# Retention and a cosine-gated MLP in one kernel: S, Y and A issued as one block on quarters of the array, later blocks with swapped key halves, and a reordered plan

## The chip, the core and the metric

The kernel runs on one core of a Trainium2 chip. The metric is the device time of the kernel in microseconds, as the median of several runs; lower is better. The profile is one further execution, recorded by the hardware.

## What is computed

q, k and v have 4 batches, 8 heads, 768 positions and 64 features. Each head keeps a 64x64 state that decays by a factor gamma at each position:

```python
for t in range(S):
    state = gamma[None, :, None, None] * state + np.einsum('bhd,bhe->bhde', k[:, :, t], v[:, :, t])
    y[:, :, t] = scale * np.einsum('bhd,bhde->bhe', q[:, :, t], state)
```

The result, as 3072 tokens of 512 features, goes through an MLP: `h = x @ w_in` (512 to 2048), `g = h * cos(h)`, `g @ w_out` (2048 to 512).

## The kernel before

**Tiling.** The sequence is cut into chunks of 128 positions. One position p of the kernel is one chunk of two batches, with all eight heads; there are 12 of them, p = 0 to 11, in the order of `ORDER`. Within a chunk the recurrence becomes matrix products: A (keys times queries, then masked so that a query sees no later key), Y (what the state before the chunk gives, plus values times masked A), and S (the state after the chunk, keys times values). Decay is put into q and v by the factors `gq` and `gk` at their conversion to bf16. Two positions make 512 tokens, a group g; six groups go through the MLP in units: an F unit (4 matmuls with 128 hidden features, `f_mm` L472; `h_mm` L493 does the same for 256 tokens and 256 features), its cosine on ScalarE (`f_cos` L480), its product on VectorE (`f_mul` L484, `h_mul` L501), and O units of four matmuls (`o_mm` L517).

**Block of a position.** `y1_mm` issues the state part of Y (L428) and the first half of the rest (`intra`, L414): keys 64 to 127 of batch 1 on the upper row half of the array, keys 0 to 63 of batch 0 on the lower. `hop` (L437) puts an empty instruction on another engine, SP up to p=5 and POOL after, that waits for this half and lets the other half follow[...]. Then come A of the next position (`a_mm` L366), the second half of Y (`y2_mm`) and S (`s_mm`, L460); in the plan at p=2 and 3 A stands apart and S comes before the second half. A and Y use quarters of the array (64 rows, 64 columns); S uses all 128 rows and half of the columns. A's second key half is computed for all 128 queries, Y's second key half for the last 64 only. ScalarE copies Y to `xt` (`y_copy`), VectorE copies the state (`s_copy`) and masks A (`a_mask`, L372).

**Order.** All instructions are ordered by hand. Up to position 5 and the first group's outputs a `Plan` orders them: each operation is added with its engines, its estimated cost, what it comes after, a rank and the tokens (PSUM banks, semaphores) that it takes and gives; `Plan.run` simulates the engines, taking the ready operation of the lowest rank, and `emit` issues the operations in the order of the simulated starts. `jitter` adds random amounts to the ranks. `HALF0` is how many of the 16 hidden blocks of the first group are computed per position rather than for both at once. `LOADS` is the order in which POOL issues the loads, each 512 KB of q, k, v or the weights. After the plan a loop goes over groups g = 2 to 6 and 16 steps: an F unit of group g, an O unit of group g-1, and at the fourth and twelfth step the block of a position, then `conv` of p+2 (keys on ScalarE, queries and values on POOL) and loads of p+4 on SP. Positions from 6 on are transposed by DMA on SP (`dma_t`, L326), the others on TensorE (`t_mm`, L337). There are seven PSUM banks, taken in turn, and one for the state. The last 128 tokens' output is computed in two halves of 256 columns (`last_o`, L537), one copied by ScalarE and one by VectorE.

Of the kernel before, what the change touches and what calls it, by code (L numbers as in the profile page):

```python
# [29 lines left out]
class Plan:  # L30
# [33 lines left out]
    def run(self, start, cold_until=0.0, look=0.0, fill=None, hold=""):  # L64
# [7 lines left out]
        while left:  # L72
            nxt = []
            for e in "SPADE":
# [6 lines left out]
                for op in left:  # L81
# [12 lines left out]
                    for k, n in op["take"]:  # L94
                        tk = sorted(self.tokens[k])
                        n += op["spare"] if k == "bank" else 0
                        if len(tk) < n:
                            ok = False
                        elif tk[n - 1] > t + 1e-9:
                            nxt.append(tk[n - 1])  # L100
                            ok = False
# [50 lines left out]
    def jitter(self, seed, by):  # L152

        r = random.Random(seed)
        for op in self.ops:
            op["rank"] += by * r.random()
# [6 lines left out]
SEED, JIT, HOLD = 60, 4.0, "PD"  # L163
HALF0, SPARE, RF, RM, COLD = 4, 1, 40.0, 40.0, 5.2
# [3 lines left out]
def kernel(  # L168
# [11 lines left out]
    C = 128  # L180
# [12 lines left out]
    ORDER = [0, NC] + [x for x in range(1, NP) if x != NC]  # L193
    LATE = NC
# [39 lines left out]
    mask = sb([128, 128], BF16, "mask")  # L234
# [3 lines left out]
    gk = sb([128, NC, H], FP32, "gk")  # L238
# [27 lines left out]
    def load(eng, p, names):  # L266

        bp, c = divmod(ORDER[p], NC)
        for n in names.split():
            t, src = SRC[n[0].lower()]  # L270
            if len(n) == 1:
# [4 lines left out]
                        "b h t d -> t (b h) d"))  # L276
            else:
# [33 lines left out]
    def conv_v(p, b, e):  # L311
        ENG[e].tensor_tensor(out=vb(p)[:, b], in0=vf[p % PRE][:, b],  # L312
                             in1=bc(gk, ORDER[p] % NC), op=ALU.mult)
# [39 lines left out]

    def a_mm(p, u):
        n = p % NB
        bk = held["a", p, u] = [banks.take(), banks.take()]
        ap = [t.rearrange("p (a t) -> p a t", a=HP) for t in bk]
        for a in range(HP):
            h = 4 * u + a
            for x in range(1 if p < 2 else 2):  # L360
                for b in range(2):
                    if p < 2:
                        nc.tensor.matmul(ap[b][:, a, :], lhsT=kt(n, b, h), rhs=qt(n, b, h),
                                         tile_position=(64 * b, 0))
                        continue
                    nc.tensor.matmul(ap[b][ts(x, 64), a, :], lhsT=kt(n, b, h)[:, ts(x, 64)],  # L366
                                     rhs=qt(n, b, h), tile_position=(64 * b, 64 * x),
                                     skip_group_check=True)

    def a_mask(p, b, u):  # L370
# [3 lines left out]
            in1=(dec[:, b] if p < 2 else mask.unsqueeze(1).to_broadcast([128, HP, 128])),  # L374
# [34 lines left out]
    def intra(p, b, a, x, **kw):  # L409

        ms = []
        for j in range(2):
            h = 2 * a + j
            ms.append(nc.tensor.matmul(  # L414
# [473 lines left out]
```

## Time and profile before

| | us |
|---|---|
| median of 7 runs | 210.26 |
| lowest, highest | 209.81, 211.09 |
| the profiled execution's own time | 210.37 |
| its span, first to last instruction | 208.6 |

Where the engines' work lies, from the groups of instructions:

| line, engine | what | count | mean ns |
|---|---|---|---|
| L472 PE | F units, 512 wide | 289 recorded | 379 |
| L517 PE | O units, 512 wide | 360 recorded | 379 |
| L493 PE | half F units, 256 wide | 160 | 273 |
| L366 PE | A | 320 | 218 |
| L414 PE | Y, values times A | 320 | 205 |
| L428 PE | Y, from the state | 160 | 222 |
| L460 PE | S | 160 | 199 |
| L480 ACT | cosines | 96 | 690 |
| L484 DVE | products | 76 | 688 |
| L372 DVE | masks | 46 | 679 |

A matmul's length in the profile runs from its start to its modelled end and overlaps those of its neighbours; starts of consecutive 512-wide ones lie 216 ns apart. In group rows the last numbers are the busy time, the mean length of one, and the idle time before it with what ended it. Some matmul records are missing, so counts can fall short of the program's.

### The profile page before, as it was taken

To read this page: it belongs to the slowest core of one execution; us is meant where nothing else is said; L and a number is where in the kernel's file an instruction comes from. 1 tells how busy PE (TensorE), PEld (TensorE's weight loads), DVE (VectorE), ACT (ScalarE), POOL (GpSimd) and SP (SyncE) were. 2 spreads that over 40 slices of the span, in tenths; PEclk is the share of its full clock that TensorE was granted. 3 is DMA by queue.
4 is the path that set the end of the run, shared out by engine and by line. 5 is a ranking of instruction groups with operands and counts; after the bars stand their busy time and mean duration, and the time that the engine had idled before them with its cause. 6 is when DMAs were issued, how large, how long until landed. Compare 5 with 4: busy or idle time off the path is not lost.

```text
span 208.6 us, 4799 instructions
## 1 busy us (share of the span) xinstructions
PE 201.4 (97%) x1994; PEld 108.9 (52%) x2017; DVE 107.7 (52%) x186; ACT 116.0 (56%) x194; POOL 80.0 (38%) x84
## 2 busy tenths in 40 slices
PE   7999999999999999999999999999999999999993
PEld 2447456789555545455455455454444444444462
DVE  5374988977725647438438438338332334443000
ACT  7677788579655456556556556554545553553120
POOL 8789989999999007007007007000000000000000
PEclk9999999999999999999999999999999999999999
DMA  7999999999999699999993502401101101110222
GB/s 121 186 258 227 306 248 294 207 335 343 342 290 175 158 234 204 249 220 236 210 265 39 173 0 54 150 0 57 50 3 50 50 10 44 50 50 21 79 79 76
DMA packets 57495, 32.05 MB, mean 154 GB/s; under 512 B 46592, under 2 KB 51968, under 8 KB 57472
## 3 DMA queue, kind: packets, MB, share of 16 engines
q0 software_dynamic: 14352, 15.47, 33.6%
q1 hardware_dynamic: 42976, 16.13, 32.6%
q8 instruction: 16, 0.26, 0.5%
q10 hardware_dynamic: 144, 0.13, 0.2%
q14 instruction: 7, 0.06, 0.1%
HBM read 27.26 MB, written 6.29 MB: 161 GB/s over the span
## 4 chain that ended last, share of the span: by engine, by line
PE 91%; DMA 4%; POOL 2%; issue 1%; DVE 0%; POOLq 0%; DVEq 0%
PE bank L517 38%; PE bank L472 31%; PE bank L493 8%; DMA vf<-in_v_dram 4%; PE bank L366 3%; PE bank L414 2%; PE st_ps L460 2%; PE bank L337 2%; PE bank L537 2%; PE bank L428 2%; PE bank L546 1%; POOL ks L273 1%; PE bank L395 1%; POOL qs L273 1%; POOL kx L273 1%
## 5 line engine op out<-in xcount | busy, mean ns | idle before, releaser
L480 ACT ACTIVATE cosb<-bank,halfpi 128x512 bf16<-128x512 f32 x96 | 65.6, 690 | 57.2 <-PE bank L472 46.2
L517 PE MATMUL bank<-w_out_sb,gt 128*128 128x512 bf16 x360 | 90.1, 379 | 0.9 <-issue 0.3
L484 DVE TENSOR_TENSOR gt<-bank,cosb 128x512 bf16<-128x512 f32 x76 | 51.6, 688 | 55.3 <-ACT cosb L480 55.3
L472 PE MATMUL bank<-xt,w_in_sb 128*128 128x512 bf16 x289 | 74.9, 379 | 0.6 <-issue 0.2
L517 PEld LDWEIGHTS <-gt 128*128 128x128 bf16 x368 | 35.6, 98 | 42.3
L472 PEld LDWEIGHTS <-w_in_sb 128*128 128x128 bf16 x304 | 29.0, 98 | 33.8
L308 POOL TENSOR_TENSOR qs<-qf,gq 128x512 bf16<-128x512 f32 x18 | 18.5, 1044 | 45.0 <-PE bank L414 44.9
L372 DVE TENSOR_TENSOR am<-bank,mask 128x512 bf16<-128x512 f32 x40 | 24.8, 679 | 0.3 <-PE bank L366 0.3
L312 POOL TENSOR_TENSOR vs<-vf,gk 128x512 bf16<-128x512 f32 x22 | 22.7, 1044 | 1.1 <-DMA vf<-in_v_dram 0.9
L297 ACT COPY ob<-bank 128x512 f32<-128x512 f32 (+1 forms) x24 | 13.9, 577 | 15.5 <-PE bank L517 14.0
L493 PE MATMUL bank<-xt,w_in_sb 128*128 128x256 bf16 x160 | 18.8, 273 | 0.0
L297 ACT CAST xt<-bank 128x512 bf16<-128x512 f32 x24 | 12.9, 589 | 9.6 <-PE bank L414 9.0
L501 DVE TENSOR_TENSOR gt<-bank,cosb 128x512 bf16<-128x512 f32 x20 | 13.5, 687 | 8.8 <-ACT cosb L480 8.8
L493 PEld LDWEIGHTS <-w_in_sb 128*128 128x128 bf16 x160 | 15.4, 98 | 2.7
L299 DVE CAST stb<-st_ps 128x512 bf16<-128x512 f32 x10 | 6.9, 687 | 11.1 <-PE st_ps L460 11.1
L297 ACT CAST ks<-kf 128x512 bf16<-128x512 f32 x20 | 11.5, 629 | 0.0
L546 PE MATMUL bank<-zero 128*128 128x512 bf16 x33 | 10.3, 439 | 1.1 <-DVE halfpi L562 1.1
L273 POOL DMA_DIRECT2D vf<-in_v_dram x8 | 9.5, 1194 | 0.0
L297 ACT COPY qkt<-bank 128x512 bf16<-128x512 bf16 x13 | 7.1, 594 | 3.1 <-PE bank L337 2.8
L414 PE MATMUL bank<-am,vs 64*64 64x64 bf16 (+1 forms) x320 | 8.3, 205 | 0.1
L299 DVE COPY ob<-bank 128x256 f32<-128x256 f32 x1 | 0.4, 424 | 13.4 <-PE bank L537 13.4
L366 PE MATMUL bank<-qkt 64*64 64x128 bf16 x320 | 7.2, 218 | 0.0
(59 smaller groups left out, 108.8 us busy)
## 6 DMA issues: line engine op xcount, KB each, us to landing
out_dram<-ob SPq DMA_DIRECT2D x23, 256.0 KB, 2.3
vf<-in_v_dram POOLq DMA_DIRECT2D x8, 512.0 KB, 9.3
qf<-in_q_dram POOLq DMA_DIRECT2D x6, 512.0 KB, 10.6
kf<-in_k_dram POOLq DMA_DIRECT2D x6, 512.0 KB, 10.4
w_out_sb<-in_moe_w_out_dram POOLq DMA_DIRECT2D x4, 512.0 KB, 12.4
qf<-in_q_dram SPq DMA_DIRECT2D x4, 512.0 KB, 4.6
kf<-in_k_dram SPq DMA_DIRECT2D x4, 512.0 KB, 6.3
vf<-in_v_dram SPq DMA_DIRECT2D x4, 512.0 KB, 6.5
```

The costliest lines, as they stand in the source:

```text
L273: eng.dma_start(out=t.rearrange("p b h d -> p (b h) d"), in_=src[ds(2 * bp, 2), :, ds(c * C, C), :].rearrange("b h t d -> t (b h) d"))
L297: nc.scalar.copy(out=out, in_=in_)
L308: ENG[e].tensor_tensor(out=qb(p)[:, b], in0=qf[p % PRE][:, b], in1=bc(gq, ORDER[p] % NC), op=ALU.mult)
L312: ENG[e].tensor_tensor(out=vb(p)[:, b], in0=vf[p % PRE][:, b], in1=bc(gk, ORDER[p] % NC), op=ALU.mult)
L366: nc.tensor.matmul(ap[b][ts(x, 64), a, :], lhsT=kt(n, b, h)[:, ts(x, 64)], rhs=qt(n, b, h), tile_position=(64 * b, 64 * x), skip_group_che ...
L372: nc.vector.tensor_tensor(out=am[p % 2][b][u], in0=bank.rearrange("p (a t) -> p a t", a=HP), in1=(dec[:, b] if p < 2 else mask.unsqueeze(1 ...
L472: nc.tensor.matmul(bank, lhsT=w_in_sb[:, i, ts(f, 128)], rhs=xt[g % 2][:, i, :], start=(i == 0), stop=(i == KIN - 1))
L480: nc.scalar.activation(out=cb, in_=bank, func=AF.Sin, bias=halfpi)
L484: nc.vector.tensor_tensor(out=gt[g % 2][:, f, :], in0=bank, in1=cb, op=ALU.mult)
L493: nc.tensor.matmul(bank[:, ts(e, 256)], lhsT=w_in_sb[:, i, ts(f + e, 128)], rhs=xt[g % 2][:, i, ts(hf, 256)], start=(i == 0 and e == 0), s ...
L501: nc.vector.tensor_tensor(out=gt[g % 2][:, f : f + 2, ts(hf, 256)], in0=bank.rearrange("p (f t) -> p f t", f=2), in1=cb.rearrange("p (f t) ...
L517: nc.tensor.matmul(bank, lhsT=gt[g % 2][:, f, ts(j, 128)], rhs=w_out_sb[:, f, :], start=(f == 0), stop=(f == KOUT - 1))
```

## The change

- Y, S and the next position's A are built as lists of quarter matmuls, one list for each row half, and `quarters` issues them in turn, each time the one whose quarter is free first by its own reckoning. S is 32 matmuls on quarters in place of 16 on half columns, in two parts with a hop of their own. Hops go over SP up to p=4 and over POOL after.
- A's second key half is computed for the last 64 queries only. From p=8 on (`SWAP`) half of the heads have their two key halves exchanged, so that each quarter gets as many wide matmuls as the others; k and v of these positions are loaded in exchanged order by six transfers each (`ks`, `vs`), and `gk3` and `mask[1]` hold factors and mask in the exchanged order, made by five small transfers on SP (`first_swapped`).
- The plan: fixed shifts of ranks and engines by operation name in place of random ones, HALF0 8 in place of 4, no hold, another order of the loads from `o1` on, a token rule that lets a block of six banks start up to 0.5 us before the last ones come free, new costs, other engines for some copies and conversions, and the transposes of p=6 and 7 after the load of k of p=7. The loads of p=8 go into the plan.
- The loop: conversions after the output's DMA; loads of p+3 in place of p+4, values a half group after queries and keys.
- `last_o` divides its columns 384 and 128.

The diff, cut to its core:

```diff
...
+                            continue
+
+                        at = max(tk[n - 1] - 0.5, tk[n - 3]) if n > 5 else tk[n - 1]
+                        if at > t + 1e-9:
+                            nxt.append(at)
                             ok = False
...
-    def jitter(self, seed, by):
-
-        r = random.Random(seed)
+    def shift(self, by, on):
+
         for op in self.ops:
-            op["rank"] += by * r.random()
+            op["rank"] += by.get(op["name"], 0.0)
+            op["engines"] = on.get(op["name"], op["engines"])
...
-SEED, JIT, HOLD = 60, 4.0, "PD"
-HALF0, SPARE, RF, RM, COLD = 4, 1, 40.0, 40.0, 5.2
+HOLD = ""
+SHIFT = {"ml010": 25.5, "mulf0.2": -74.7, "f0.3": 0.3, "cosf0.2": -11.6,
...
+ON = {"cv70": "P", "cv00": "D", "cv30": "D", "cv31": "D", "cv60": "D", "cv11": "D",
...
+HALF0, SPARE, RF, RM, COLD = 8, 1, 50.0, 50.0, 5.2
...
+    SWAP = 8
...
-    gk = sb([128, NC, H], FP32, "gk")
+    gk3 = sb([128, 5 * NC * H], FP32, "gk3")
+    gk = gk3[:, : NC * H].rearrange("p (c h) -> p c h", c=NC)
...
+            elif n[1] == "s":
+                fl = t[p % PRE].rearrange("p b h d -> p (b h) d")
+                for x in range(2):
+                    for lo, n4, th in ((0, 4, x), (4, 8, 1 - x), (12, 4, x)):
+                        eng.dma_start(
+                            out=fl[ts(x, 64), ds(lo, n4), :],
+                            in_=src[ds(2 * bp, 2), :, ds(c * C + 64 * th, 64), :]
+                            .rearrange("b h t d -> t (b h) d")[:, ds(lo, n4), :])
...
+        if p >= SWAP:
+            n = NC * H
+            g = gk3[:, ds(b * n + ORDER[p] % NC * H, 2 * n + 8)].rearrange("p (u r) -> p u r", u=2)
+            ENG[e].tensor_tensor(
+                out=vb(p)[:, b].rearrange("p (u x) d -> p u x d", u=2),
+                in0=vf[p % PRE][:, b].rearrange("p (u x) d -> p u x d", u=2),
+                in1=g[:, :, :HP].unsqueeze(3).to_broadcast([128, 2, HP, D]), op=ALU.mult)
+            return
...
+    def second(p, x, b, u):
+        return x ^ (u ^ b if p >= SWAP else 0)
+    def a_banks(p, u):
+        bk = held["a", p, u] = [banks.take(), banks.take()]
+        return [t.rearrange("p (a t) -> p a t", a=HP) for t in bk]
+    def a_one(p, ap, u, a, b, x):
+        h, lo = 4 * u + a, 64 * second(p, x, b, u)
+        return nc.tensor.matmul(
+            ap[b][ts(x, 64), a, lo:], lhsT=kt(p % NB, b, h)[:, ts(x, 64)],
+            rhs=qt(p % NB, b, h)[:, lo:], tile_position=(64 * b, 64 * x), skip_group_check=True)
...
+    def quarters(rows):
+        free = [[0.0, 0.0], [0.0, 0.0]]
+        left = [list(r) for r in rows]
+        while left[0] or left[1]:
+            best = None
+            for r in range(2):
+                for c in range(2):
+                    nxt = next((m for m in left[r] if m[0] == c), None)
+                    if nxt:
+                        t = max(free[r][c], nxt[2])
+                        if best is None or t < best[0]:
+                            best = (t, r, nxt)
+            t, r, m = best
+            left[r].remove(m)
+            free[r][m[0]] = t + m[1] / 2.4
+            m[3]()
+        return max(max(f) for f in free)
+    def hop_on(p):
+        return nc.sync if p <= 4 else nc.gpsimd
+    def y_part(p, r, part):
+        b = r ^ part
+        out = []
+        for a in range(HP):
+            for j in range(2):
+                h = 2 * a + j
+                lo = 64 * second(p, r, b, h // 4)
+                def fn(a=a, j=j, h=h, lo=lo):
+                    m = nc.tensor.matmul(
+                        held["yp", p][b][ts(j, 64), a, lo:], lhsT=vs[p % NB][ts(r, 64), b, h, :],
+                        rhs=am[p % 2][b][h // 4][ts(r, 64), h % 4, lo:],
+                        start=False, stop=True, tile_position=(64 * r, 64 * j),
+                        skip_group_check=True)
+                    told("y", p, part, m)
+                out.append((j, 128 - lo, 0.0, fn))
+        return out
+    def y_inter(p, b):
+        out = []
+        for a in range(HP):
+            for j in range(2):
+                def fn(a=a, j=j, h=2 * a + j):
+                    m = nc.tensor.matmul(
+                        held["yp", p][b][ts(j, 64), a, :], lhsT=stb[p % 2][ts(b, 64), h, :],
+                        rhs=qt(p % NB, b, h), start=(a == 0), stop=False,
+                        tile_position=(64 * b, 64 * j), skip_group_check=True)
+                    told("y", p, 0, m)
+                out.append((j, 128, 0.0, fn))
+        return out
+    def s_part(p, r):
+        x = 1 if p == LATE else p
+        out = []
+        for h in range(H):
+            for b in range(2):
+                def fn(h=h, b=b):
+                    m = nc.tensor.matmul(
+                        st_ps[ts(b, 64), h, :], lhsT=kb(x)[ts(r, 64), b, h, :],
+                        rhs=vb(x)[ts(r, 64), b, h, :],
+                        start=(ORDER[x] % NC == 0 and h == 0 and r == 0), stop=True,
+                        tile_position=(64 * r, 64 * b), skip_group_check=True)
+                    told("s", p, r, m)
+                out.append((b, 64, 0.0, fn))
+        return out
+    def a_rows(p, b):
+        return [(x, 128 - 64 * second(p, x, b, u), 0.0,
+                 lambda a=a, u=u, x=x: a_one(p, held["ap", p][u], u, a, b, x))
+                for u in range(2) for a in range(HP) for x in range(2)]
+    def told(what, p, part, m):
+        key = (what, p)
+        if part == 0:
+            held.setdefault(("ms", key), []).append(m)
+            if len(held["ms", key]) == (32 if what == "y" else 16):
+                w = held["hop", key] = hop_on(p).nop(nofuse=True)
+                for x in held.pop(("ms", key)):
+                    after(x, w)
+        elif held.get(("first", key), 0) < 4:
+            held["first", key] = held.get(("first", key), 0) + 1
+            after(held["hop", key], m)
+    def late(ms, t):
+        return [(c, n, t, fn) for c, n, _, fn in ms]
+    def y_block(p, a_next):
         bk = [banks.take(), banks.take()]
         held["y", p, 0], held["y", p, 1] = bk
         held["yp", p] = [t.rearrange("p (a t) -> p a t", a=HP) for t in bk]
+        if a_next:
+            bk = [[banks.take() for u in range(2)] for b in range(2)]
+            for u in range(2):
+                held["a", p + 1, u] = [bk[1][u], bk[0][u]]
+            held["ap", p + 1] = [[t.rearrange("p (a t) -> p a t", a=HP)
+                                  for t in held["a", p + 1, u]] for u in range(2)]
+        rows = []
+        t1 = sum(m[1] for m in y_inter(p, 0) + y_part(p, 0, 0)) / 4.8 + 250
+        t2 = sum(m[1] for m in y_inter(p, 0) + y_part(p, 0, 0) + s_part(p, 0)) / 4.8 + 250
+        for r in range(2):
+            ms = y_inter(p, r) + y_part(p, r, 0)
+            if has_s(p) and r == 0:
+                ms += s_part(p, 0)
+            if a_next:
+                ms += a_rows(p + 1, r)
+            ms += late(y_part(p, r, 1), t1)
+            if has_s(p) and r == 1:
+                ms += late(s_part(p, 1), t2)
+            rows.append(ms)
+        return quarters(rows)
+    def has_s(p):
+        return p != 1 and (p == LATE or ORDER[p] % NC < NC - 1)
...
+        for i, (lo, n) in enumerate(((0, 384), (384, 128))):
             bank = banks.take()
             for f in range(KOUT):
-                nc.tensor.matmul(bank[:, :256], lhsT=gt[g % 2][:, f, ts(j, 128)],
-                                 rhs=w_out_sb[:, f, ts(hf, 256)],
+                nc.tensor.matmul(bank[:, :n], lhsT=gt[g % 2][:, f, ts(j, 128)],
+                                 rhs=w_out_sb[:, f, ds(lo, n)],
                                  start=(f == 0), stop=(f == KOUT - 1))
-            copy("AD"[hf], o[:, ts(hf, 256)], bank[:, :256])
-            (nc.sync, nc.scalar)[hf].dma_start(
-                out=out[ds(o_row(g, j), C), ts(hf, 256)], in_=o[:, ts(hf, 256)])
+            copy("AD"[i], o[:, ds(lo, n)], bank[:, :n])
+            (nc.sync, nc.scalar)[i].dma_start(
+                out=out[ds(o_row(g, j), C), ds(lo, n)], in_=o[:, ds(lo, n)])
...
-    CQ, CD = "D", "P"
-    SPLIT = {(1, 1, 0), (0, 1, 1)}
+    CQ, CD = "P", "DP"
+    SPLIT = {(1, 1, 1), (0, 1, 1)}
...
+                                    [T["c" + x, p, 0], T["c" + x, p, 1], ld["k", 7, 0]] + old, 10 * p,
...
-            def y(e, p=p, a_next=a_next):
-                y1_mm(p)
-                hop(p)
-                if a_next:
-                    a_mm(p + 1, 0)
-                    a_mm(p + 1, 1)
-                    y2_mm(p)
-                if has_s(p):
-                    s_mm(p)
-                if not a_next:
-                    y2_mm(p)
-            o = add("E", 0.66 + 0.445 * a_next + (0.35 if a_next else 0.45) * has_s(p), y,
+            o = add("E", (1.4 if a_next else 1.2) if has_s(p) else 1.15 if a_next else 0.85,
+                    lambda e, p=p, a_next=a_next: y_block(p, a_next),
                     ym[0] + ym[1] + sm, 10 * p + 3, [("bank", 6 if a_next else 2)], (), "quad",
...
+    def first_swapped(e):
+        n = NC * H
+        for x in range(2):
+            nc.sync.dma_start(out=gk3[ts(x, 64), ds(n, n)], in_=gk3[ts(1 - x, 64), :n])
+            nc.sync.dma_start(out=mask[1][ts(x, 64), :], in_=mask[0][ts(1 - x, 64), :])
+        nc.sync.dma_start(out=gk3[:, ds(2 * n, n)], in_=gk3[:, :n])
+    add("S", 3.0, first_swapped, [T["cv", 1, 0]], 30, name="sw")
+    add("S", 8.0, lambda e: load(nc.sync, PL + 2, "q ks vs"),
+        [T["dt", PL + 1, w] for w in range(2)], 10 * PL + 20, name="l8")
...
-    for p in (PL + 2, PL + 3):
-        load(nc.sync, p, "q k v")
...
     def block(p):
         nxt = p + 1 < NP
-        y1_mm(p)
-        hop(p)
-        if nxt:
-            a_mm(p + 1, 0)
-            a_mm(p + 1, 1)
-        y2_mm(p)
+        y_block(p, nxt)
         for b in range(2):
             y_copy(p, b, "A")
         if has_s(p):
-            s_mm(p)
             s_copy(p, "D")
         if nxt:
             for u in range(2):
...
                 o_out(g - 1, s // 4, "A")
             if p < NP and r == 3:
                 block(p)
-                if p + 2 < NP:
-                    conv(p + 2)
-                if p + 4 < NP:
-                    load(nc.sync, p + 4, "q k v")
             if s % 4 == 3:
                 o_dma(g - 1, s // 4)
+            if p + 2 < NP and r == 3:
+                conv(p + 2)
+            if p + 3 < NP and s % 4 == 3:
+                load(nc.sync, p + 3, "q ks" if r == 3 else "vs")
```

## The prediction

> **What bounds the kernel now.** I read the page first, then the windows by stage, then the timeline of the stretches that the change touches. The page:
>
> ```profile
> PE 201.4 (97%) x1994; PEld 108.9 (52%) x2017; DVE 107.7 (52%) x186; ACT 116.0 (56%) x194; POOL 80.0 (38%) x84
> ...
> PE   7999999999999999999999999999999999999993
> ...
> PEclk9999999999999999999999999999999999999999
> ...
> PE 91%; DMA 4%; POOL 2%; issue 1%; DVE 0%; POOLq 0%; DVEq 0%
> ```
>
> TensorE is busy from slice 2 to slice 39 at the full granted clock, and 91% of the chain that ended last is its own work. The stages (columns: window, length, then busy us and count for each engine, clock, DMA share, GB/s):
>
> ```profile
> 16.00:70.00 54.00, 53.26 (x763) 36.40 (x768) 37.18 (x63) 37.76 (x65) 50.77 (x50) 1.00 1.15 277
> 70.00:201.40 131.40, 130.50 (x1077) 62.80 (x1092) 61.52 (x94) 65.75 (x105) 16.22 (x16) 1.00 0.41 103
> ```
>
> Both stages leave TensorE under 1% idle. In the planned stage (16 to 70) POOL comes next with 50.8 of 54 us, in the loop nothing comes near. So the time is a sum of TensorE work, plus a start fed by loads and a tail. Only TensorE work removed counts, as long as nothing makes TensorE wait; it takes its instructions in order, so each wait is paid in full.
>
> **One attention block now.** The timeline of TensorE around the block of position p=6 (start, length, engine, line):
>
> ```profile
> 76.60 1.03 PE L517 MATMUL bank<-w_out_sb,gt 128*128 128x512 bf16 x4
> ...
> 77.56 0.42 PE L428 MATMUL bank<-qkt,stb 64*64 64x128 bf16 x16
> ...
> 77.81 0.33 PE L414 MATMUL bank<-am,vs 64*64 64x128 bf16 x14
> ...
> 77.99 0.69 PE L366 MATMUL bank<-qkt 64*64 64x128 bf16 x30
> ...
> 78.47 0.43 PE L414 MATMUL bank<-am,vs 64*64 64x128 bf16 x16
> ...
> 78.83 0.44 PE L460 MATMUL st_ps<-vx,kx 128*64 128x64 bf16 x16
> ...
> 79.20 1.04 PE L472 MATMUL bank<-xt,w_in_sb 128*128 128x512 bf16 x3
> ```
>
> A matmul's length includes its way through the array, so I read starts. Four 512-wide ones in 1.03 us, each 0.379 long, start 0.216 apart: the last leaves the array free at 76.60 + 4x0.216 = 77.46. The block ends where L472 starts, 79.20: 1.74 us. There are three changes of tiling (before L428, before L460, before L472), each about 0.09 empty. L428 is four rounds of four quarters; the next line starts 0.25 after it, 80 ns for the first round and 55.5 for the others, so a 128-wide quarter matmul costs 55.5 ns. L460 has eight rounds of two 64-wide ones: its last start is 0.44 - 0.20 = 0.24 after its first, 50 ns for the first step and 32 for the other six. A 64-wide one costs 32 ns with its own weight load, not half of 55.5.
>
> In the other blocks (ends found in the same way): p=2 1.61 (0.19 of it a wait inside Y), p=3 1.37, p=4 1.71, p=5 1.73, p=7 to 10 1.74 each, p=11, which has no S and no next A, 1.18:
>
> ```profile
> 155.39 0.42 PE L428 MATMUL bank<-qkt,stb 64*64 64x128 bf16 x16
> 155.63 0.91 PE L414 MATMUL bank<-am,vs 64*64 64x128 bf16 x32
> 156.47 0.82 PE L472 MATMUL bank<-xt,w_in_sb 128*128 128x512 bf16 x2
> ```
>
> Here the hop, the semaphore that lets the second half of Y follow the first, is bare: 0.91 less the 0.43 of two halves and the last matmul's 0.216 leaves about 0.27 of waiting.
>
> **The change, part by part.**
>
> *Blocks.* S goes onto quarters (32 matmuls of 64 in place of 16 of 128 rows), so two of four tiling changes on the way go: before, full to quarter to half to full (0.28); after, in and out (0.19). A's second key half covers only the columns that survive the mask (64). A block lasts as long as its fullest quarter. For p=4,5,6 the halves are not swapped (SWAP is 8): row 0, column 0 has state part 4, first half of Y 4, A 8, second half 4, all 128-wide: 20x55.5 = 1.11; S adds 8x32 = 0.26; with 0.025 for the first round and 0.19: 1.58. Gains 0.13, 0.15, 0.16, together 0.45. p=7 computes the swapped A of 8: 16x55.5 + 12x32 = 1.27, plus 0.21, is 1.48: 0.26. In p=8,9,10 swapping makes all quarters equal, 12x55.5 + 16x32 = 1.18, plus 0.21, is 1.39: 0.35 each, 1.06. Hops are covered there by S and A (0.6 between the halves against 0.27). p=11: 0.25 + 0.175 + 0.27 + 0.175 + 0.19 = 1.06: 0.12. In p=2 and 3 there is no A to cover a hop, and S now waits for one itself: 0.47 for the first part of Y, 0.26 for half of S, 0.27 waiting, 0.28 for the rest, 0.19, about 1.48: p=3 loses 0.11, p=2 gains about as much where its inner wait goes. **Blocks: -1.89.**
>
> *A rule against this.* The Trainium skill, "TensorEngine Tiling (Array Packing)", Restrictions, says column tiling turns fast weight load off, and "TensorE: Matmul & The Clock Gate", LDWEIGHTS, prices a load at columns/1.2 ns: 64 columns, 53 ns. If a quarter couldn't hide its own load, 64-wide work would cost 53, and swapped blocks 12x55.5 + 16x53 + 211 = 1.72: nothing gained. The L460 row, column-tiled too, steps by 32 ns with a new load each. I take 32. What no row shows is four quarters at 32 ns for long: the block has 112 matmuls and as many loads in 1.2 us, 5.3 ns an instruction, where the densest stretch here (77.81 to 78.11, 28 pairs) has 5.4. At the mean pace of the present quarter part (160 in 1.18 us, 7.4) a swapped block would take 1.87. Below 1.39 it can't go. Nearest is the dense stretch, so 1.39.
>
> *Tail.* The last 128 columns are split 384/128 in place of 256/256:
>
> ```profile
> 205.13 0.42 DVE L299 COPY ob<-bank 128x256 f32<-128x256 f32 x1 [13.36 <-PE bank L537]
> 205.59 0.37 ACTq L541 DMA_DIRECT2D out_dram<-ob  x1
> ...
> out_dram<-ob ACTq DMA_DIRECT2D x1, 128.0 KB, 1.8
> ```
>
> TensorE's sum stays (transposes of 128 columns show 55.5 each, so 16x0.163 + 16x0.056 = 3.49 as now). The final copy halves: a 128x128 f32 DVE row of the start took 0.29, so -0.13. The transfer halves: 256 KB land in 2.3, 128 KB in 1.8, so 64 KB in about 1.6, -0.2. The 384 part is out about 0.3 before. I take **-0.3** (0 to -0.4).
>
> *Plan.* HALF0 8 in place of 4 replaces four full units (0.864) by four of 256-wide matmuls (0.873): +0.04. The reordering can't make TensorE denser than dense: what is there to win is the fill and the wait before 17 us (0.6 at most, as w_in's first piece lands at 15.4 and the load order up to there is the same) and p=2's wait. It can lose: I bound it by -0.5 and +3, and take 0, since the work that moves is the same and the loads up to o1 keep their order. The swapped mask and gk are five small transfers on SP, in a stretch where SP has 2 to 4 things to do in 10 us; hidden. The loads of p=8 on become 13 issues for 3 on SP, same bytes; SP issued a load in 0.4 to 3.2 us and is idle half of the loop. In the loop p+3 is loaded instead of p+4: its q and k go out after block p and landed 4.6 to 7.5 us after issue, needed 15.6 later; its v half a group later, still some 4 us before its conversion. Hidden; without the cover ScalarE's conversion would hold up the cosines behind it. POOL's hops for p=5 and now also for S queue behind POOL's conversions (1.04 each); POOL's last one of this stage ended at 67.94, where p=5's hop is wanted at about 68.0. Nothing to 0.5; I take 0. y copies start about 0.35 later against the block's end, which one output unit (0.86) just covers if both engines share them, as the plan now allows for several.
>
> **Sum:** -1.89 - 0.3 + 0.04 = -2.15 on the profiled execution's 210.37 (span 208.6): 208.2. Its time lies 0.11 over the median 210.26, so **208.1**.
>
> **Rivals.**
> (a) *Blocks don't shrink*: loads or issue rate cost 64-wide work 50 ns or more. Then blocks give -0.1 to +0.4, the tail -0.3: about 210.2. For it: the rule, and no sustained row. Against it: the 32 ns steps.
> (b) *The end of the plan comes late; slower.* The transposes of p=6 now wait until k of p=7 has landed (61.99). Now the second is issued at 62.8 and lands at 67.65, and block p=5 starts at 67.96. With 0.45 saved before it, TensorE arrives at about 67.4. Both transposes after 62.0, 1.3 of SP each and 4.8 to land, give 68.1, a stall of 0.7, and SP standing behind any output first gives more; then y copies and the next group's first unit follow serially. Slower than before once p=5 starts after 69.6, some 2.2 late; if loads slip by 1.5 as well it starts at 70.4 and the time is 211.1. For it: the 94% busy POOL that issues the loads. Against it: sixteen output units that can be put ahead of the block.
> (c) *The plan gains too*: 0.6 at the start and 0.2 in p=2 give 207.3.
> (d) *The title's "iotas first"* has no line in the diff, and swapping reaches only p=8 on; if swapping paid nothing, four blocks would be at 1.58: 208.9, within the forecast.
>
> **How the numbers follow.** Forecast (207.6 to 209.5) 0.60, (c) 0.10, (a) 0.13, (b) 0.17. A change under 0.3%, 0.63 us, can't be told from none. (a) divides 0.03 faster, 0.08 same, 0.02 slower, (b) 0.02, 0.02, 0.13. So faster 0.75, same 0.10, slower 0.15. The range leaves out half of (b) and the far end of (c): 206.8 to 210.7.
>
> **What would show it.** Swapped blocks at 1.39 between full units, p=4 to 6 at 1.58, p=3 near 1.48; no TensorE gap over 0.1 at block p=5 or after it; last copy 0.29. A 64-wide step well over 32 ns is (a); a gap before p=5 or before the first unit of group 2 is (b).

## The result and the profile after

The change makes the kernel faster, by less than half of what was forecast. The median goes from 210.27 to 209.33 us; the ratio is 0.9955, with a 95% interval of 0.9943 to 0.9968. That is 0.94 us gained, where the forecast was 2.17. The profiled execution took 209.19 us with a span of 207.4, against 210.37 and 208.6 before.

The page of the changed kernel, first its busy times, then TensorE's rows by slices, then the chain of waits by engine:

```profile
PE 200.2 (97%) x2154; PEld 109.5 (53%) x2178; DVE 113.7 (55%) x194; ACT 115.7 (56%) x193; POOL 73.4 (35%) x77
...
PE   7999999999999999999999999999999999999994
...
PEclk9999999999999999999999999999999999999999
...
PE 83%; DMA 8%; POOL 3%; issue 2%; ACT 2%; DVE 1%; POOLq 0%; DVEq 0%; ACTq 0%
```

The clock is as before and TensorE is as dense, so nothing happened to the speed of the engine. But its own work is 83% of the chain where it was 91, and DMA has 8% where it had 4: more of the chain runs over loads. (In e2 below, which is faster, these shares are 74 and 12%, so they don't measure a loss.) The stages, cut as before (columns: window, length, busy us and count for PE, PEld, DVE, ACT and POOL, clock, DMA share, GB/s):

```profile
16.00:70.00 54.00, 52.90 (x848) 38.25 (x852) 42.32 (x69) 38.13 (x65) 44.14 (x43) 1.00 1.08 273
70.00:201.40 131.40, 130.23 (x1161) 62.47 (x1176) 61.26 (x94) 66.58 (x106) 16.35 (x16) 1.00 0.41 106
```

POOL has lost 6.6 us of the planned stage, TensorE stands 0.36 us more there, 1.10 in place of 0.74. These rows don't tell how much work was done by 70 us, so the account has to be made piece by piece. Below, a block is the time from the end of the unit before it to the start of the unit after it, as in the prediction:

| block | before | forecast | after |
|---|---|---|---|
| p=2, p=3 | 1.61, 1.37 | 1.48, 1.48 | 1.45, 1.45 |
| p=4 | 1.71 | 1.58 | 1.60 |
| p=5 | 1.73 | 1.58 | **1.84** |
| p=6 | 1.74 | 1.58 | 1.69 |
| p=7 | 1.74 | 1.48 | 1.52 |
| p=8, 9, 10 | 1.74 each | 1.39 each | 1.50, 1.48, 1.43 |
| p=11 | 1.18 | 1.06 | 1.11 |

The blocks gave 1.23 of the 1.89 expected, 0.08 of it in p=2 to 5 and 1.15 in p=6 to 11. What else moved in the two profiles: TensorE's start on the second of the first two positions' Y products (`y_first`, L431; L395 before) is at 15.69 in place of 15.45 (+0.24), a filling matmul at 16.9 went (-0.22), a new wait stands before A of p=2 (+0.18), a new gap before group 2's first unit (+0.35), and the tail, from the start of the last output to the end of the span, is 6.66 in place of 7.21 (-0.55, forecast -0.3). Together with the half units (+0.04) this makes -1.2, the difference of the spans.

### The profile page after: what moved, and what is told of

It is laid out like the page before. It is cut to its first block, busy times and chain, and to the rows that moved or that the text cites. A ratio compares the mean times of both kernels' runs of the same rounds, so it can differ in the third digit from the quotient of the medians.

```text
span 207.4 us, 5205 instructions
## 1 busy us (share of the span) xinstructions
PE 200.2 (97%) x2154; PEld 109.5 (53%) x2178; DVE 113.7 (55%) x194; ACT 115.7 (56%) x193; POOL 73.4 (35%) x77
## 4 chain that ended last, share of the span: by engine, by line
PE 83%; DMA 8%; POOL 3%; issue 2%; ACT 2%; DVE 1%; POOLq 0%; DVEq 0%; ACTq 0%
PE bank L635 38%; PE bank L590 28%; PE bank L611 7%; DMA kf<-in_k_dram 4%; DMA vf<-in_v_dram 4%; PE bank L480 2%; PE bank L389 2%; PE bank L494 2%; PE bank L655 2%; PE st_ps L508 1%; PE bank L361 1%; POOL ks L281 1%; POOL am L420 1%; POOL qf L281 1%; POOL qs L281 1%
## 5 line engine op out<-in xcount | busy, mean ns | idle before, releaser
L590 PE MATMUL bank<-xt,w_in_sb 128*128 128x512 bf16 x274 | 71.4, 379 | 0.8 <-ACT xt L313 0.2
L590 PEld LDWEIGHTS <-w_in_sb 128*128 128x128 bf16 x288 | 27.5, 98 | 32.5 <-issue 0.5
L611 PE MATMUL bank<-xt,w_in_sb 128*128 128x256 bf16 x192 | 22.3, 273 | 0.1
L611 PEld LDWEIGHTS <-w_in_sb 128*128 128x128 bf16 x192 | 18.5, 98 | 3.1
L313 ACT CAST xt<-bank 128x512 bf16<-128x512 f32 x21 | 11.4, 588 | 9.0 <-PE bank L480 8.3
L480 PE MATMUL bank<-am,vs 64*64 64x128 bf16 (+1 forms) x320 | 10.3, 206 | 0.1
L331 POOL TENSOR_TENSOR vs<-vf,gk 128x512 bf16<-128x512 f32 x8 | 8.2, 1042 | 5.6 <-DMA vf<-in_v_dram 4.0
L336 POOL TENSOR_TENSOR vs<-vf,gk 128x512 bf16<-128x512 f32 x8 | 8.3, 1048 | 2.9 <-PE bank L480 2.1
L315 DVE CAST stb<-st_ps 128x512 bf16<-128x512 f32 x9 | 6.2, 687 | 5.7 <-PE st_ps L508 4.8
L389 PE MATMUL bank<-qkt 64*64 64x64 bf16 (+1 forms) x320 | 8.3, 207 | 0.3 <-DVE qkt L315 0.3
```

What stands on the lines that cost most here:

```text
L313: nc.scalar.copy(out=out, in_=in_)
L389: return nc.tensor.matmul(ap[b][ts(x, 64), a, lo:], lhsT=kt(p % NB, b, h)[:, ts(x, 64)], rhs=qt(p % NB, b, h)[:, lo:], tile_position=(64 * ...
L480: m = nc.tensor.matmul(held["yp", p][b][ts(j, 64), a, lo:], lhsT=vs[p % NB][ts(r, 64), b, h, :], rhs=am[p % 2][b][h // 4][ts(r, 64), h % 4 ...
L590: nc.tensor.matmul(bank, lhsT=w_in_sb[:, i, ts(f, 128)], rhs=xt[g % 2][:, i, :], start=(i == 0), stop=(i == KIN - 1))
L611: nc.tensor.matmul(bank[:, ts(e, 256)], lhsT=w_in_sb[:, i, ts(f + e, 128)], rhs=xt[g % 2][:, i, ts(hf, 256)], start=(i == 0 and e == 0), s ...
```

## The experiments

Twelve kernels ran, in three groups (e1, e6, e7 and e8; e2 to e5; e9 to e12); each ratio is against the kernel before on the same chip at the same time. e1, e2 and e4 rest on four runs each, the others on six to twelve.

| kernel | median | ratio | interval |
|---|---|---|---|
| e1, no swapped halves | 209.45 | 0.9963 | 0.9949 to 0.9977 |
| e2, swapped tables made later | 208.97 | 0.9921 | 0.9901 to 0.9941 |
| e3, hops of p=4 on POOL | 209.41 | 0.9958 | 0.9941 to 0.9975 |
| e4, Y copies of p=5 on two engines | 208.80 | 0.9925 | 0.9904 to 0.9945 |
| e5, plan of before, new loop and tail | 208.67 | 0.9915 | 0.9900 to 0.9930 |
| e6, measured costs in `quarters` | 209.45 | 0.9957 | 0.9940 to 0.9974 |
| e7, even tail | 209.84 | 0.9972 | 0.9958 to 0.9986 |
| e8, e2 + e3 + e4 | 208.46 | 0.9909 | 0.9891 to 0.9928 |
| e9, e8 + e6 | 208.52 | 0.9921 | 0.9904 to 0.9939 |
| e10, swapped tables made three times | 210.99 | 1.0039 | 1.0021 to 1.0057 |
| e11, the changed kernel again | 209.73 | 0.9981 | 0.9966 to 0.9997 |
| e12, e5 + e6 | 208.46 | 0.9917 | 0.9899 to 0.9934 |

e11 sets the scale. It is the changed kernel itself, was expected at 0.994 to 0.997, and gives 0.9981 where the first measurement gave 0.9955: half a microsecond can lie between two groups of runs. Differences of that size between groups are not read as effects here.

### The plan against the rest: e5

The plan of before (its ranks, engines, loads, and its blocks of p=2 to 5) is put under the new loop and the new tail.

```diff
-    plan.shift(SHIFT, ON)
+    plan.jitter(SEED, JIT)
     plan.emit()
+    first_swapped("S")
+    load(nc.sync, PL + 2, "q ks vs")
```

> The plan of before (random ranks, half units up to 4, blocks p=2 to 5 as before, A alone half wide) with the loop's new blocks (p=6 to 11), swapped loads and the new tail. Theory (the planned stage gives back the gain): the blocks p=6 to 11 keep the 1.15 us that they saved (0.05, 0.22, 0.25, 0.26, 0.31, 0.07), the dense start comes back to 15.45, no wait before group 2: 208.4 or less. Rival (the new blocks themselves make what follows late): a wait before or after the blocks appears here too and the time stays at 209.3 or above.

It is faster than the changed kernel: 0.9915, 1.77 us under the kernel before in its group. The loop's terms and the tail were forecast at 1.60 + 0.3 = 1.9 together, so they came out within 0.13 of the forecast. The plan's terms (blocks p=2 to 5, half units, everything at the start) were forecast at -0.25. By the difference of the ratios, 0.9955 - 0.9915 of 210.3 us, they are **+0.84** (about +-0.4 from the intervals). Inside one group the difference is as large or larger: e3, the new plan with a mend that shows no gain, lies 0.90 over e5, and e11 lies 1.3 over e12, the old plan again. Nearly the whole shortfall lies in the plan; the next three experiments look for it there. (e5 also takes the five small transfers out of the start, so their price is in this number.)

### The small transfers at the start: e2 and e10

The DMA view of the changed kernel from 0 to 16 us, by queue (packets, MB, share of 16 engines) and by issue (count, KB each, median us to landing):

```profile
q1 hardware_dynamic: 2544, 0.61, 18.2%
...
w_in_sb<-in_moe_w_in_dram POOLq DMA_DIRECT2D x2, 256.0 KB, 8.5
...
gk<-gk SPq DMA_DIRECT2D x2, 12.0 KB, 6.1
mask<-mask SPq DMA_DIRECT2D x2, 16.0 KB, 6.0
gk<-gk SPq DMA_DIRECT2D x1, 24.0 KB, 6.8
```

The plan meant the five swapped tables (`first_swapped`) for about 14 us. Nothing stands before them on SP and their wait is met from the start, so SP issued them from 5.2 to 7.7 us, among the loads on which the whole start depends. They carry 80 KB, less than a sixth of one load, but took 6 to 7 us each to land. e2 lets them come after block p=2, at 33 us:

```diff
-    add("S", 3.0, first_swapped, [T["cv", 1, 0]], 30, name="sw")
+    add("S", 3.0, first_swapped, [T["y", 2, 0]], 30, name="sw")
```

> As after, the five small transfers of first_swapped put behind the first hops on SP (about 33 us) instead of at 5 us. Theory (they take turns with the first loads): v of p=0 and 1 and the first piece of w_in land 0.1 to 0.2 earlier, the dense start moves from 15.69 to 15.45, about -0.2 in time. Rival (the start is late for its new order of casts and masks): landings move, the start doesn't, no change in time.

The same view of e2:

```profile
q1 hardware_dynamic: 2080, 0.52, 14.4%
...
w_in_sb<-in_moe_w_in_dram POOLq DMA_DIRECT2D x2, 256.0 KB, 7.8
```

The packets of the five took 3.8% of all sixteen engines' time in 16 us, as the profile counts it; that isn't yet a delay, since packet times overlap (the two queues of the changed kernel, 121.1 and 18.2%, add up to 139%). The weight loads land 0.7 us sooner without them. The timeline of TensorE where it becomes dense, first of the changed kernel (start, length, engine, line), then of e2:

```profile
15.69 0.64 PE L431 MATMUL bank<-am,gt 128*64 128x128 bf16 x16
16.26 1.92 PE L611 MATMUL bank<-xt,w_in_sb 128*128 128x256 bf16 x16
```

```profile
15.32 0.64 PE L431 MATMUL bank<-am,gt 128*64 128x128 bf16 x16
15.89 1.92 PE L611 MATMUL bank<-xt,w_in_sb 128*128 128x256 bf16 x16
```

The first F unit starts 0.37 earlier. The time, 0.9921, is below both measurements of the changed kernel by 0.7 and 1.3 us. But the start also differs between executions of kernels that are the same up to there (e11 began L431 at 15.96 and then waited 1.07 for the second piece of `w_in`), so one profile can't carry this. All fourteen together can: in the eight with the five transfers at the start this product begins at 15.45 to 16.13, in the mean at 15.81, and POOL's queue has moved 2.36 to 2.43 MB of loads by 16 us; in the six without them it begins at 15.32 to 15.74, in the mean at 15.50, with 2.44 to 2.50 MB. So about 0.3 us of the price shows at the start; where the rest of e2's gain lies isn't shown. e10 gives three times the dose, in one group with e11:

```diff
-        for x in range(2):
+        for again in range(3):
+            for x in range(2):
```

> As after, with the five transfers of first_swapped issued three times in a row at the start (the same data each time). The start of dense work was 15.45 to 16.13 in six profiles with them early and 15.32 to 15.51 in four without: overlapping. Theory (they take turns with the first loads): with fifteen of them the first piece of w_in lands at 16.0 or later, the dense start at 16.1 or later, the time 0.4 to 0.9 over that of after in the same job. Rival (start times scatter by themselves): dense start still between 15.4 and 16.1, no change in time.

It takes 210.99, slower than the kernel before, and 1.26 us more than e11 (difference of the ratios 0.0058, about +-0.0024 from their intervals). Ten more transfers of 12 to 24 KB cost some 0.12 us each. They didn't cost it at the first F unit, where it was expected: SP issued them from 10.8 to 21 us, and L431 began at 15.86. SP had nothing else to do until the first hop at 33 us, so its queue is not what made the kernel longer. The loads are: from 16 to 32 us POOL's queue (q0) moved 0.37 MB less than in the changed kernel (4.17 in e11), for 0.15 MB of small transfers. e10, then the changed kernel:

```profile
q0 software_dynamic: 3123, 3.79, 113.4%
q1 hardware_dynamic: 845, 0.15, 8.2%
```

```profile
q0 software_dynamic: 3193, 4.16, 120.5%
```

Against the first profile of the changed kernel the loss is in transposes at 27.5 that took 1.26 in place of 0.89 because a conversion was late, in a gap at 43.4 that is 0.25 longer, and in a block p=5 with 2.25 us from its first to its last quarter in place of 1.66, though this length varies as much without the extra ten (next section). (The profile of e11 can't be set beside it, by the 1.07 at its start.) By the rate from the times the first five cost 0.6, an estimate, since the extra ten came later.

### Block p=5 and the hops of p=4: e3

The timeline of TensorE at block p=5 of the changed kernel, and after it to the first unit of group 2:

```profile
68.09 0.42 PE L494 MATMUL bank<-qkt,stb 64*64 64x128 bf16 x16
68.34 0.33 PE L480 MATMUL bank<-am,vs 64*64 64x128 bf16 x14
...
68.69 0.22 PE L389 MATMUL bank<-qkt 64*64 64x128 bf16 x2
...
70.06 0.81 PE L635 MATMUL bank<-w_out_sb,gt 128*128 128x512 bf16 x3 [0.16 <-issue]
71.07 0.59 PE L590 MATMUL bank<-xt,w_in_sb 128*128 128x512 bf16 x2 [0.19 <-ACT xt L313]
```

And SP before it:

```profile
63.23 1.34 SPq L350 DMA_TRANSPOSE qkt<-ks  x1
64.74 3.14 SPq L350 DMA_TRANSPOSE qkt<-qs  x2
```

A of p=6 (L389) needs both transposes. The first is issued at 63.23, after SP has stood in the two hops of p=4 until 63.11 (k of p=7 had landed at 60.93); the second is issued at 64.74. Its landing is not in this trace; in eight other profiles of the new plan A starts 0.04 to 0.05 us after it, which puts it at about 68.65 here. The plainest of them is e7, which has this part of the plan unchanged:

```profile
68.37 0.33 PE L480 MATMUL bank<-am,vs 64*64 64x128 bf16 x14
69.29 0.22 PE L389 MATMUL bank<-qkt 64*64 64x128 bf16 x2 [0.59 <-DMA qkt<-qs]
```

This is the stall of rival (b), in the middle of the block in place of before it. e3 takes the hops of p=4 off SP:

```diff
-        return nc.sync if p <= 4 else nc.gpsimd
+        return nc.sync if p <= 3 else nc.gpsimd
```

> As after, the two hops of p=4 on POOL instead of SP. Theory (the transposes of p=6 are late because SP stands in these hops): they are issued about 0.8 us earlier, the wait of 0.24 in block p=5 goes, block 1.60 instead of 1.84; -0.2 in time. Rival (the transposes are late because k of p=7 lands at 60.9 and DMA is full): issued earlier, they land as late, the wait stays.

In the profile it does what it should:

```profile
62.48 1.34 SPq L350 DMA_TRANSPOSE qkt<-ks  x1
64.00 3.53 SPq L350 DMA_TRANSPOSE qkt<-qs  x2
```

The block's quarters take 1.49 us in place of 1.66. With the hop of p=4 on SP this length was 1.58 to 2.25 in eight runs (1.66, 1.94, 1.96, 2.23, 1.95, 1.72, 2.25, 1.58), with it on POOL 1.49, 1.52 and 1.39. From the block's start to A it is 0.56 to 1.20 us in these eight, and 0.44, 0.37 and 0.38 with the hop on POOL; so A waits 0.2 to 0.8, 0.5 in the mean, and the first profile of the changed kernel, with 0.2, is a lucky one. The time of e3 alone, 0.9958, shows no gain over the changed kernel. The block is shorter, but by no more than two groups differ.

### The gap before group 2: e4

In the rows of the changed kernel at block p=5 the last O unit leaves the array at 70.71 (four from 69.85, one of them missing in the record) and F starts at 71.07, released by ScalarE's `xt`. The Y copies of p=5, both on ScalarE (columns as before; the last bracket is ScalarE's own idle time):

```profile
69.94 1.07 ACT L313 CAST xt<-bank 128x512 bf16<-128x512 f32 x2 [2.89 <-PE bank L480]
```

Two of about 0.54 in a row end at 71.01. Before, the two copies began while the block still ran, and F followed O without a gap:

```profile
69.44 1.07 ACT L297 CAST xt<-bank 128x512 bf16<-128x512 f32 x2 [2.42 <-PE bank L414]
69.91 0.81 PE L517 MATMUL bank<-w_out_sb,gt 128*128 128x512 bf16 x3 [0.16 <-issue]
70.56 1.02 PE L472 MATMUL bank<-xt,w_in_sb 128*128 128x512 bf16 x4
```

Since Y's second half is now the last thing in the block, both halves come free at its end, and one O unit of 0.86 can't cover two copies and their waits. e4 puts one on VectorE:

```diff
-"yc50": 39.8
+"yc50": -60.0
...
-"yc50": "DA"
+"yc50": "D"
```

> As after, one of the two copies of Y of p=5 on VectorE ahead of its masks instead of both on ScalarE. Theory (group 2's first unit waits for two copies in a row that start when the last half of Y is done): the 0.355 before it goes to under 0.1, -0.3 in time. Rival (VectorE's masks move back by 0.6 and something behind them waits instead): the gap moves, no change.

In the profile F follows O at once, one matmul (missing in the record) after the third:

```profile
70.62 0.81 PE L635 MATMUL bank<-w_out_sb,gt 128*128 128x512 bf16 x3 [0.16 <-issue]
71.27 1.03 PE L590 MATMUL bank<-xt,w_in_sb 128*128 128x512 bf16 x4
```

The gap is 0.36 in all eight profiles of the new plan with both copies on ScalarE, and 0.01 or less in the three with this edit and the three of the old plan. The time is 0.9925, 0.6 below the first measurement of the changed kernel. The gap itself explains 0.36 of that.

### All three: e8, with measured costs: e6, e9 and e12

e8 has the edits of e2, e3 and e4.

> As after, with the three edits together: first_swapped's transfers late, the hops of p=4 on POOL, Y of p=5 copied by two engines. Theory (the planned stage loses its part at three places of its own): dense start near 15.4, block p=5 under 1.70, no gap before group 2; together 0.7 to 0.9 under after, ratio to before about 0.992 or less. Rival (each only moves the lateness to the next): one of the gaps comes back and the ratio stays at 0.9935 or more.

It gives 0.9909, 1.81 us under the kernel before. Against the first measurement of the changed kernel that is 1.0, where the three alone gave about 0.7, 0 and 0.6; within the half microsecond between groups this agrees. e8 and e5 can't be told apart: the mended new plan is as good as the old one, not better.

The other lead was the blocks of the loop. `quarters` reckons 128/2.4 and 64/2.4, 53 and 27 ns; the traces show 55.5 and 32. e6 gives it these numbers:

```diff
-            free[r][m[0]] = t + m[1] / 2.4
+            free[r][m[0]] = t + cost(m)
```

where `cost` is 55.5 for 128 columns and 32.0 for 64, and `t1` and `t2` follow.

> As after, but the order of the quarter matmuls reckoned with the measured 55.5 and 32 ns and 280 ns for a hop in place of 53.3, 26.7 and 250. Theory (blocks are longer than their fullest quarter because TensorE stands in order behind a hop that isn't through): p=6 goes from 1.51 to about 1.40 between its first and last quarter, p=7 from 1.34 to 1.29, p=8 and 9 from 1.30 to 1.24; -0.3 in time. Rival (224 instructions in 1.2 us are too many for the issue): lengths stay.

A miss for the most part. The quarters of p=4 and 6 shrink from 1.41 and 1.51 to 1.39 each, those of p=7 and 8 grow a little (1.34 to 1.40, 1.31 to 1.34), and the time is 0.9957. With the mends, and on the old plan, it brings nothing either:

> The three mends (late first_swapped, hops of p=4 on POOL, Y of p=5 by two engines) with the measured quarter costs. If the parts add up: p=4 and p=6 at 1.39, p=5 at 1.5 or less, no gap before group 2, ratio to before 0.988 to 0.991. If the mends only shift lateness, it stays at the 0.991 of the mends alone or above.

> The plan of before with the new loop and the measured quarter costs. The plan of before has no wait in block p=5 and none before group 2: ratio 0.990 to 0.992 as without the costs, p=6 at 1.39 instead of 1.55. If the new plan's blocks p=2 to 5 are worth their 0.3 once its waits are mended, the other kernel, with the three mends, is faster by about that; if not, this one is.

0.9921 and 0.9917, like e8 and e5. Beside e11 in the same group they are 1.2 and 1.3 us faster than the changed kernel. The timeline of e9 at block p=5 shows the two mends working, with no gap after 69.40 + 4x0.216:

```profile
67.90 0.42 PE L497 MATMUL bank<-qkt,stb 64*64 64x128 bf16 x16
...
69.61 0.81 PE L638 MATMUL bank<-w_out_sb,gt 128*128 128x512 bf16 x3 [0.16 <-issue]
70.26 1.03 PE L593 MATMUL bank<-xt,w_in_sb 128*128 128x512 bf16 x4
```

### The swapped halves: e1

```diff
-    SWAP = 8
+    SWAP = 12
```

and the loads in plain order.

> As after, but no position has swapped key halves (plain loads, plain mask and factors from p=8 on). Theory (a block lasts as long as its fullest quarter): p=8, 9 and 10 go from 1.25 to 1.31 up to about p=6's 1.4 to 1.5, p=7 from 1.34 to 1.45, together +0.6 to +0.8 in time. Rival (swapping buys nothing, since issue or hops set the length): no change.

In its profile the quarter parts of p=6 to 10 are all 1.42 us. Over p=7 to 11 they sum to 6.69, and to 6.11 in the changed kernel: swapping is worth 0.58 us of TensorE in the profile. The time, 0.9963 against 0.9955, is 0.2 us longer where 0.6 to 0.8 was expected; it doesn't show the gain, nor exclude it (both intervals are +-0.3 us, and the groups differ).

### The uneven tail: e7

```diff
-        for i, (lo, n) in enumerate(((0, 384), (384, 128))):
+        for i, (lo, n) in enumerate(((0, 256), (256, 256))):
```

> As after, but the last 128 tokens' columns divided 256 and 256 as before. Theory of the prediction (copy and transfer of the last part): from the start of the last output matmuls to the end of the span 6.66 becomes 6.9, +0.23 in time. Rival (the 0.55 that the tail lost comes from the order of the waits at the end of the program): it stays at 6.7.

The last output's matmuls (L655; L537 before), the last copy and the issue behind it, of the changed kernel and of e7:

```profile
200.74 3.66 PE L655 MATMUL bank<-w_out_sb,gt 128*128 128x384 bf16 x32
...
204.49 0.29 DVE L315 COPY ob<-bank 128x128 f32<-128x128 f32 x1 [13.36 <-PE bank L655]
204.81 0.37 ACTq L659 DMA_DIRECT2D out_dram<-ob  x1
```

```profile
201.33 3.66 PE L655 MATMUL bank<-w_out_sb,gt 128*128 128x256 bf16 x32
...
205.08 0.42 DVE L315 COPY ob<-bank 128x256 f32<-128x256 f32 x1 [13.36 <-PE bank L655]
205.53 0.37 ACTq L659 DMA_DIRECT2D out_dram<-ob  x1
```

The copy takes 0.29, to the digit what was forecast. From the start of the last output to the end of the span e7 needs 6.87 and the changed kernel 6.66: the split is worth 0.21 in these profiles, not the whole 0.55 that the tail gained. (In the times e7 lies 0.36 over the first measurement of the changed kernel, less than groups differ.) The rest, 0.34, is there in e7 too. Before, where this output starts at 201.38, SP runs through six waits of about 0.06 each after the last transfer has landed (207.38 to 207.74); in the changed kernel and in e7 it goes through all but one of them earlier. Five waits are 0.30 of the 0.34. No run has the old order of the waits with the rest of the new kernel, so this is read from the traces alone.

## Why the prediction was right in its sign and wrong in its size

**What held.** That the time is a sum of TensorE's work, and that the sign follows from the blocks: the loop and the tail alone give -1.77 (e5), forecast -1.9. That these two come so near is partly luck: in the profiles the loop's blocks fell 0.45 short and the tail gave 0.25 more. p=2 to 4 came within 0.04 of their forecast. The last copy was right, and so was the tail's sum for the split (0.21 by e7, within the 0 to -0.4 that was given).

**The rule and the rows.** The sum took 32 ns for a 64-wide quarter matmul, and not the 53 that one estimates from the Trainium skill's price of a weight load ("TensorE: Matmul & The Clock Gate", LDWEIGHTS). The swapped block p=8 decides it for 32, on four quarters, where no row of before could:

```profile
109.18 0.34 PE L480 MATMUL bank<-am,vs 64*64 64x128 bf16 x16
109.35 0.20 PE L508 MATMUL st_ps<-vs,ks 64*64 64x64 bf16 x2
109.36 0.22 PE L389 MATMUL bank<-qkt 64*64 64x64 bf16 x2
109.38 0.20 PE L508 MATMUL st_ps<-vs,ks 64*64 64x64 bf16 x2
109.39 0.19 PE L389 MATMUL bank<-qkt 64*64 64x64 bf16 x1
109.41 0.20 PE L508 MATMUL st_ps<-vs,ks 64*64 64x64 bf16 x2
```

S, on the two quarters of one row half, steps by 0.03 with a new load each, while A runs on the other row half beside it. p=10 has its 112 matmuls (48 of them 128 wide, 64 of them 64) and as many loads in 1.25 us, where its fullest quarter needs 1.20. At 53 ns its block would take 1.72 by the prediction's sum; it took 1.43. Rival (a) is out.

**Failed step: "five small transfers on SP, in a stretch where SP has 2 to 4 things to do in 10 us; hidden".** The cover was looked for on SP, and SP was indeed idle. What they displaced was on the sixteen DMA engines, where the start's loads were queued. They also ran at 5 us and not where the plan had them. Their price is 0.3 us by the start in fourteen profiles, 0.6 at e10's rate and 0.7 or more by e2's time; none of the three is sharper than a few tenths. This is the part that was named with no cost if the cover is gone.

**Failed step: the plan "can lose: I bound it by -0.5 and +3, and take 0", and with it block p=5 at 1.58.** It was 1.84. Rival (b) had the mechanism, both transposes of p=6 late on SP, though what held them last was SP's hops of p=4 ("SP standing behind any output first gives more") and not k of p=7. It priced this at a stall of 0.7 before the block. Its sum has a slip: it lets 0.45 be saved before block p=5, but that is the sum for p=4, 5 and 6; before p=5 come p=2 to 4 with 0.15, so TensorE arrives at 67.8 and the stall is 0.3. In the first profile it cost 0.26: A comes second in the block, and the second transpose landed some 3.9 us after its issue and not 4.8. Over the eight profiles the wait is 0.2 to 0.8, 0.5 in the mean, at 3.8 to 4.5 us to landing. It was given as a rival and not as a term of the sum; nothing spoke against the wait itself, only against its size.

**Failed step: y copies start later "which one output unit (0.86) just covers if both engines share them".** The condition was written down and not looked up. The plan gives one of the two copies of p=5 to ScalarE in any case; the table `ON` leaves the other, `yc50`, to the scheduler, and with its rank it went to ScalarE too. The price is 0.35 and e4 takes it away.

**Mis-sized term: the loop's blocks, -1.60 against -1.15 in the profile.** That hops "are covered there by S and A" and that a block "lasts as long as its fullest quarter" gives a lower bound. A hop takes 0.31 to 0.33 us from the last start before it to the first after it (p=2, 3 and 11), and TensorE takes its instructions in one order, so where a quarter waits for one the other three stand too: at p=6 no quarter starts anything for 0.10 until the hop of S is through. p=8 and 9 lasted 0.1 longer than their fullest quarter, p=10 only 0.04. Between profiles with swapped halves p=7 to 9 vary from 1.25 to 1.44 in their quarter part, and e6 was to end this and didn't: **why they vary stays open**. So does the value of the new order once mended; it lies within what e5 and e8 can't tell apart.

**Mis-sized term: the tail, -0.3 against -0.55**, by the order of the waits at the end of SP's program, which no row in the prediction named. The forecast part measured 0.21; the other 0.34 was in no term.

In sum, in the profile: blocks short by 0.66, group 2's gap 0.35, start and A of p=2 0.20, tail better by 0.25: 0.96 short of 2.15. In the times, e5 puts 1.1 of the 1.2 into the plan. The profiles agree with that once their means are taken, an estimate: start 0.31, wait in p=5 0.49 and gap 0.36 are losses of 1.16; with the plan's other pieces (filling matmul -0.22, A of p=2 +0.18, half units +0.04, blocks p=2 to 4 -0.19, p=5 without its wait -0.12) they make +0.85, where e5 has +0.84; so near an agreement is luck, with +-0.4 on e5. (The forecast for all these was -0.25.) Rival (d)'s "iotas first" stands in no title here and plays no part. The best kernels are e5, e8, e9 and e12 at about 208.5 us.

## What to carry to other kernels

A transfer is hidden only if neither its queue nor the DMA engines are short at the time when it is really issued, and an instruction whose wait is already met on an idle queue is issued at once, not when a plan means it. A condition that a forecast writes down ("if both engines share them") has to be looked up or priced. When a large change gains little, undo its larger part as a whole (here the plan) before single suspects, since this tells in which part the loss lies.

## What the runs showed of the hardware that was not expected

- Small transfers among the loads have a price out of proportion to their bytes: with 80 KB in five at the start dense work began 0.3 us later (the mean of eight profiles against that of six without them), and ten more, 0.15 MB, kept 0.37 MB of loads from moving in 16 us and lengthened the kernel by 1.26 us (e10 against e11).
- 64-wide matmuls on quarters go on at 32 ns each with a weight load of their own while the other quarters work: a block of 112, 64 of them 64 wide, took 1.25 us.
- The two DMA transposes of p=6 took SP 1.24 and 1.34 us to issue, and the one that A waits for landed 3.8 to 4.5 us after its issue began in the new plan's profiles, so the order of SP's queue decided how long block p=5 stood.
- The waits at the end of SP's program take about 0.06 us each, so five of them after the last landing and not before it are 0.30 us of the kernel's time.
